# Loading `a` in pairs of chunks for chunks 4 to 11, a third PSUM bank for `b`, and new instruction orders in a scan-plus-adapters kernel

## The chip, the core and the metric

The kernel runs on one core of one Trainium2 chip. A core has a matrix engine (TensorE, PE), a vector engine (VectorE, DVE), a scalar engine (ScalarE, ACT), a general engine (GpSimd, POOL) and a queue engine that here only issues transfers (SyncE, SP); sixteen DMA engines move data between HBM and the on-chip memory. The metric is the device time of one execution in microseconds (us), lower is better. A difference under 0.2%, about 0.4 us here, is hardly to be told from no change.

## The reference

Two inputs `a` and `b`, each 8 sequences of 6,400 rows of 128 numbers, go through a linear recurrence along the sequence. Its output, taken as 51,200 rows `x`, goes through a mixture of eight adapters of rank 16, of which each row uses the two with the largest gate logits:

```python
for t in range(S):
    h = a[:, t] * h + b[:, t]
    out[:, t] = h
...
logits = x @ w_gate                       # 8 logits per row
topk = the two largest per row            # K = 2
w = softmax over those two
delta = sum over the two of w * (x @ A[e]) @ B[e]
return x + delta
```

The two inputs are 26.2 MB each and the output is 26.2 MB, so at least 78.6 MB pass between HBM and the core.

## The kernel before, in words

The 51,200 rows are cut into 100 chunks of 512. A chunk goes through these steps; the letter is the kind of operation as the written orders name it, and the line is that of the profile.

- Load `a` (`x`) and load `b` (`y`), L291, issued by SP (the first `b` by ACT). `LOADS_A` says how many chunks one load of `a` covers: 1 for the first and the last four chunks, 4 for the 92 chunks between. `SEGMENTS` says it for `b`: 1 at both ends, 2 between. A chunk in a load of m is read in rows of 2 KB times m per partition. A tile has four slots of four chunks (`NL`), so loads can be 16 chunks ahead of use; a load waits until its slot's old contents have been transposed.
- Front: PE transposes the chunk so that time lies along the free dimension, L306. A chunk of `a` alone is `a`, a chunk of `b` alone is `b`; between the ends one chunk of `b` and one of `a` that lies ahead are transposed as one group, `f`. With 4-chunk loads, a group for `a` takes one half of the rows of two chunks. ACT copies the transposed `a` out of PSUM (`a`, L342).
- Scan: DVE runs the recurrence of a chunk, reading `a` from SBUF and `b` from PSUM (`s`, L358). Each scan starts from the last column of the one before, so scans are a chain.
- Logits and low-rank products: PE multiplies blocks of 128 rows, up to three at a time, by the 136 columns of A and the gate (`z`, L455) and ACT copies them out (`z`, L462).
- Gating, once for each group in `GROUPS` (1, 1, 2, 2, then 6 chunks, then 4, 2, 2, 1, 1): DVE operations `1`, `2`, `3`, `4`, `6` find the two largest logits (L487 to L503), POOL subtracts (`5`, `8`, L498 and L501), ACT takes one sigmoid (`u`, L507), POOL builds the gates (`p`, `q`, `r`, L516 to L520).
- Back: the products are multiplied by the gates (`m`, L544) on POOL or DVE, as `MU` says for each chunk (82 on POOL, 18 on DVE, these nearly all late); PE transposes two chunks of them (`t`, L552); ACT or DVE copies that out, as `TE` says for each pair (21 on ACT, 31 on DVE, L561); PE adds x and the second product (`d`, L579 and L580); ACT copies the sum out (`o`, L587).
- Store: SP issues the store of one or two chunks (`o` in its own order, L616).

Each engine runs a fixed order, written out in `ORDER` as one letter per operation. An engine takes its operations strictly in that order and waits where an operand is not ready, so a load behind a store in SP's string is issued only once that store's chunk is done. The transfers that SP issues are worked through in the order of issue.

PSUM has eight banks. Two are for transposed `b` (`BANK_B`, banks 1 and 2; a bank is free once its chunk is scanned). Six form a ring (`RING`) that `a`, `f`, `z`, `t` and `d` take in turn; an operation that takes a bank waits for the copy that empties the one six turns back.

The lines that decide which part of `a` goes with which chunk of `b`, before:

```python
if place[0][c][2] == 4 and place[0][c][3] == 0:
    for i in range(4):
        ahead[c + i] = (c + 4 + 2 * (1 - i % 2), i // 2)
```

So `f` of chunk c takes a half of two chunks of `a` from the next 4-chunk load, and a front cannot start before both its `b` and that next load of `a` have landed. The numbers `COLD`, `SOLO`, `FUSED`, `AE` and the `dur` arguments feed the search for the orders; the instructions do not depend on them.

Of the kernel before, what the change touches and what calls it, by code (L numbers as in the profile page):

```python
# [20 lines left out]
ONE_SIGMOID, T_UNIT = True, 2  # L21
RING = [0, 3, 4, 5, 6, 7]
SPLIT = {}
ORDER = {
    "pe": (
        "wwwwwbawwabwzzwwwwbwwazzbaaaazzaztffffzztzfdzzffzzfdfzfzzzffzzftzzffdzfdzzftzfzfzdfdzfzzzfzzfttzzffd"
        "dtddzzfzfdzzfztdffzzdtdffzztdzfdzzfdtzffzztddffzddtdffddzztzffzztzdffzdzztffzzzzdddtdtffzddztffzdzdf"
        "ddfztzzffzdzdtffzzzddftzzzffdztzdftfddzftddffzzzdzfzdftzzffzztzddffdztzdtffzztddffddzzzfdzztzzfzdftz"
        "zfdtdffzzzdddffdtztzffzzzddfdfttzdffazzdztdfddtzzzdzzddtafazdzzbtdzbzztddztdbzzadbdtddzdzdzttddtzddt"
        "dddtdtddddttdd"  # L30
    ),
    "act": (
        "ycciacazzazzuaaaazzuzaataaazztzzauaozzaazozaazzzzaazuatazzaoauzzoztzaazzaoazoazzzzzaauztzaaoooozzaza"
        "ozzazoaazzuootaazozzazoazozaazzutoaoazoouoaaoozzzaazztzoaazzozaazzzzooouoaazooztaazzoooaoazzzuaazzoo"
        "aazzzooazzzaaozztoautaoozaooaazzzoazzouazzaazzzooaaozztoaazzouoaaoozzzaozzzzzaoatzzauooaazzzoooaaozt"
        "zaauzzzaoooatzoaaazzuozooozzzoozzotaauzzzotozzzzoootzzauoouoozzotoztuoooztooooouuoooooo"
    ),
    "dve": (
        "ss12346ss123m4i61ss2s3s4s1s6s2s3s4s6s1s2s3s4s6sss1ss2s3s4sts16s2t3ss4sts1s62s3sts4sts1s263s4stssts6s"
        "ssts1s234tts1s263ss4ssts6sts1s2sts3s41s26s3sts4ss6sts1sts23sts4s6t1s2ssts13s4s2t6s3s4s6stss1s23sts4s"  # L40
        "m6tsts1m2m34s6ss1st12m3m4263s4ts1mm2m63m4mm6t1m21m32m34m4t66tmmtt"
    ),
    "pool": (
        "ccc85qpr85pqrmc855pqrmm8pqrmm85qprmmmm58mmqprmmmmm85mpqrmmmm85mmpqr58mmmmpmqmrmmmm85mmpqrmmm8m5mpqmr"
        "mmmmmm58qprmmm85mmmqprmmmmm58pmqrmmmmmm58pqrmm58mmmmqprmmmm58pqrmmm58qpmrmm58mq85prpq85pqrr8585ppqqr"
        "r"
    ),
    "sp": (
        "xxyxyxyxyxyxyyyxyyxyyxooyxyyoxyyyyyoxxoooyyxoyyyxoyxyooyyxoxoyoyyxoyyxyoooxyoyxyooyxyooyyxooyyxoyyxo"
        "oyxyoooyxoxxyyyoooyooooooooooooooooooo"  # L50
    ),
}
# [105 lines left out]
def bass_associative_scan_2x2__then__mixture_of_adapters_kernel(  # L158
# [21 lines left out]
    span = {}  # L180
    for m in BACKS:
        c0 = len(span)
# [5 lines left out]
    with ExitStack() as stack:  # L188
# [34 lines left out]
        g = sbuf("g", [128, GB, E], F32, NG)  # L223
# [6 lines left out]
        P = Program()  # L230
# [98 lines left out]
        def emptied(c, g, o, ba):  # L329

            ab = c % NA
            m = place[0][c][2]
            if m == 1:
                dst, src = a_st[:, ab, :], lambda: ps[:, ba.n, :]
                chunks = [c]
            else:
                assert ab + 2 <= NA
                dst = a_st[:, ab : ab + 2, :].rearrange("d m t -> d (m t)").rearrange("d (p g j) -> d g p j", g=2, j=8)[:, g, :, :]
                src = lambda: ps[:, ba.n, :].rearrange("d (p j) -> d p j", j=8)
                chunks = [c, c + 1]  # L340
            e = P.add("act", "a", [o] + [ast_user[k % NA] for k in chunks] + [o_sg if c == 0 else None],
                      lambda: eng["act"].copy(dst, src()), dur=AE[0 if m == 1 else 1])  # L342
            ba.evac = e
            for k in chunks:
                o_ae.setdefault(k, []).append(e)
# [26 lines left out]
        for c in range(NCH):  # L372
            if place[0][c][2] == 4 and place[0][c][3] == 0:
                for i in range(4):
                    ahead[c + i] = (c + 4 + 2 * (1 - i % 2), i // 2)

        def solo_a(c, g):
            ba = Bank()
            m = place[0][c][2]
            deps, ts = turned(0, c, ba, g)  # L380
            deps += [w] if c == 2 else []
            o_A[c, g] = P.add("pe", "a", deps, each(ts), dur=SOLO[min(m, 2)] * COLD.get(c, 1), lock=m > 1, ring=ba)
            used(0, c, o_A[c, g])
            emptied(c, g, o_A[c, g], ba)

        def front(c):
            P.at = c
            bb = Bank()
            bb.n = bank_b(c)
            sl, q, m, h = place[0][c]  # L390
            if m == 1:
                solo_a(c, 0)
            elif (c - h, 0) not in o_A:
                for p in (0, 2):
                    for g in (0, 1):
                        solo_a(c - h + p, g)
            deps, ts = turned(1, c, bb)
            deps += user[bb.n]
            if c in ahead and place[0][c + 4][2] == 4:
                c1, g = ahead[c]  # L400
                ba = Bank()
                deps2, ts2 = turned(0, c1, ba, g)
                o = P.add("pe", "f", deps + deps2, each(ts2, ts), dur=FUSED[2], lock=True, ring=ba)
                o_A[c1, g] = o
                used(0, c1, o)
                used(1, c, o)
                o_B[c] = o
                scanned_at(c)
                emptied(c1, g, o, ba)
            elif c in ahead:  # L410
                if h % 2:
                    return
                b2 = Bank()
                b2.n = bank_b(c + 1)
                deps2, ts2 = turned(1, c + 1, b2)
                o = P.add("pe", "f", deps + deps2 + user[b2.n], each(ts, ts2), dur=FUSED[2], lock=True)
                for k in (c, c + 1):
                    used(1, k, o)
                    o_B[k] = o
                    scanned_at(k)  # L420
            else:
                o = P.add("pe", "b", deps, each(ts), dur=SOLO[m] * COLD.get(c, 1))
                used(1, c, o)
                o_B[c] = o
                scanned_at(c)
# [11 lines left out]
        def scanned(b):  # L437
            c0, m = span[b // 4]
            return o_sc[c0 + m - 1]
# [7 lines left out]
        def zlogits(b0, n):  # L447
            P.at = (b0 + n - 1) / 4
            bk = Bank()
            z0 = zpos[b0]  # L450
            assert n <= 3

            def zmm():
                for k in range(n):
                    last = eng["pe"].matmul(ps[:, bk.n, k * W : k * W + W], xblock(b0 + k), Awg_h)  # L455
                return last

            o = P.add("pe", "z", [scanned(b0 + n - 1), o_ch], zmm, dur=(0.059 if span[b0 // 4][1] == 1 else 0.062) * n, ring=bk)
# [111 lines left out]
        def out_chunk(c, e_t):  # L570
# [12 lines left out]
            o_D[c] = P.add("pe", "d", [e_t, o_cB], delta, dur=0.448 if span[c][1] == 1 else 0.48, ring=bo)  # L583
# [39 lines left out]
            o_st.extend(parts)  # L623


        c0 = 0
        behind, due = [], []
        for gi, n in enumerate(GROUPS):
            nb = 4 * n
# [7 lines left out]
            cuts = list(zip(cut, cut[1:]))  # L637
            step = 2 if n % 2 == 0 else 1
            for c in range(c0, c0 + n, step):
                for k in range(c, c + step):  # L640
                    for i, near in ((0, 7), (1, 1)):
                        while loads[i] and loads[i][0][0] <= k + near:
                            load(i, *loads[i].pop(0))
                    front(k)
                while cuts and cuts[0][1] <= 4 * (c + step - c0):
                    k0, k1_ = cuts.pop(0)
                    zlogits(4 * c0 + k0, k1_ - k0)
                for k in range(-(-len(due) * step // (c0 + n - c))):
                    back(*due.pop(0))
# [80 lines left out]
```

## Time and profile before

| | |
|---|---|
| median of 3 runs | 203.28 us (203.04 to 203.30) |
| profiled execution | 203.03 us, of which its span is 201.2 us |
| PE / DVE / ACT / POOL busy | 179.9 / 177.1 / 178.2 / 127.4 us |
| moved by DMA | 79.28 MB, mean 394 GB/s over the span |
| mean granted PE clock | 0.987 |

The profile is of one execution, the one of 203.03 us. Its span runs from the first to the last instruction or transfer; 1.8 us of the execution's time lie outside it. Times in the rows below are us from the start of the span. A row of a group gives busy time, the mean of one instruction in ns, and the idle time of the engine just before. A row of the stretches view gives, for each engine, busy us and in brackets the number of instructions, then the granted PE clock, the share of the sixteen DMA engines that was busy, and GB/s. A row of the issues view gives the size of one transfer and the median time from its issue to its landing, that is until the last of the sixteen engines has delivered its part.

### The profile page before, as it was taken

The numbers are of one execution on the slowest core, as the hardware profiler recorded it, in microseconds if no ns is written. First come the engines' busy times: TensorE is split into PE (matmuls) and PEld (weight loads), VectorE is DVE, ScalarE is ACT, GpSimd is POOL, SyncE is SP. The second block draws the span as 40 slices with busy tenths as digits, with TensorE's granted clock in tenths as the row PEclk, the third lists the DMA queues.
The fourth block names the chain that finished last, engine by engine and source line by source line (L and its number), as shares of the span: only waits on it lengthen the run. The fifth ranks groups of instructions, "written<-read, shape, count | busy, mean of one in ns | idle before, by whom it ended". The sixth has DMA issues, their size and how long they took to land.

```text
span 201.2 us, 7662 instructions
## 1 busy us (share of the span) xinstructions
PE 179.9 (89%) x3150; PEld 164.3 (82%) x3150; DVE 177.1 (88%) x269; ACT 178.2 (89%) x384; POOL 127.4 (63%) x205
## 2 busy tenths in 40 slices
PE   4986788899989998999999999899999999898880
PEld 3975676788989998899999998789989898897760
DVE  0587689999989998999999999898999999999860
ACT  2376597999999999999999999899999999999970
POOL 1024006692797979785998697678788885865420
PEclk9999699999999999999999999999999999999998
DMA  6999999999999999999999999999999999998596
GB/s 189 396 410 414 414 410 412 416 421 396 419 415 419 409 411 423 410 423 406 419 418 405 418 415 415 416 415 414 422 410 411 415 407 404 418 360 346 234 357 226
DMA packets 21379, 79.28 MB, mean 394 GB/s; under 512 B 3424, under 2 KB 3552, under 8 KB 18400
## 3 DMA queue, kind: packets, MB, share of 16 engines
q1 hardware_dynamic: 19872, 78.39, 96.5%
q10 hardware_dynamic: 1472, 0.40, 0.9%
q8 instruction: 25, 0.41, 0.9%
q14 instruction: 10, 0.08, 0.1%
HBM read 52.56 MB, written 26.21 MB: 391 GB/s over the span
## 4 chain that ended last, share of the span: by engine, by line
PE 51%; DVE 17%; DMA 16%; ACT 5%; issue 4%; SPq 3%; POOL 2%; ACTq 0%
PE ps L306 20%; DMA b_tm<-in_b_dram 16%; DVE xT L358 10%; PE ps L455 10%; PE ps L579 8%; PE ps L552 7%; PE ps L580 6%; DVE zw L544 3%; ACT outt L587 3%; SPq L291 3%; ACT zl L462 1%; DVE zwT L561 1%; POOL g L518 1%; DVE L L492 1%; DVE k L490 0%
## 5 line engine op out<-in xcount | busy, mean ns | idle before, releaser
L358 DVE TENSOR_TENSOR_SCAN xT<-a_st,xT,ps 128x512 f16<-128x512 f32 x96 | 120.2, 1253 | 7.4 <-PE ps L306 5.3
L544 POOL TENSOR_TENSOR zw<-zl,g 128x512 f16<-128x512 f32 x82 | 85.9, 1069 | 9.9 <-PE ps L552 8.6
L306 PE MATMUL ps<-ident_f,a_tm 64*128 64x64 f32 (+1 forms) x768 | 66.3, 232 | 6.6 <-DVE xT L358 2.4
L462 ACT COPY zl<-ps 128x408 f32<-128x408 f32 (+1 forms) x138 | 67.9, 596 | 4.7 <-PE ps L455 4.5
L342 ACT COPY a_st<-ps 128x512 f32<-128x512 f32 x100 | 62.9, 691 | 7.3 <-PE ps L306 6.9
L306 PE MATMUL ps<-ident_f,b_tm 64*128 64x64 f32 (+1 forms) x768 | 66.0, 233 | 2.8 <-DMA b_tm<-in_b_dram 1.5
L306 PEld LDWEIGHTS ps<-ident_f,a_tm 64*128 64x128 f32 (+1 forms) x768 | 55.9, 141 | 13.0 <-issue 3.0
L587 ACT COPY outt<-ps 128x512 f32<-128x512 f32 x100 | 61.5, 691 | 2.9 <-PE ps L580 2.3
L306 PEld LDWEIGHTS ps<-ident_f,b_tm 64*128 64x128 f32 (+1 forms) x768 | 54.9, 141 | 4.4 <-issue 2.4
L579 PE MATMUL ps<-ident_h,xT 128*128 128x128 f16 x400 | 57.3, 231 | 0.6 <-ACT zwT L561 0.4
L580 PE MATMUL ps<-cst_h,zwT 128*128 128x128 f16 x400 | 55.7, 220 | 1.7 <-issue 1.7
L579 PEld LDWEIGHTS ps<-ident_h,xT 128*128 128x128 f16 x400 | 49.5, 142 | 3.9 <-ACT zwT L561 0.9
L580 PEld LDWEIGHTS ps<-cst_h,zwT 128*128 128x128 f16 x400 | 42.7, 107 | 1.1 <-issue 1.1
L455 PE MATMUL ps<-cst_h,xT 128*128 128x136 f16 x400 | 41.7, 232 | 1.3 <-DVE xT L358 0.9
L455 PEld LDWEIGHTS ps<-cst_h,xT 128*128 128x128 f16 x400 | 32.2, 145 | 4.2 <-DVE xT L358 1.4
L552 PE MATMUL ps<-ident_h,zw 128*128 128x128 f16 x400 | 30.8, 219 | 1.4 <-DVE k L490 0.6
L552 PEld LDWEIGHTS ps<-ident_h,zw 128*128 128x128 f16 x400 | 23.9, 98 | 3.3 <-ACT outt L587 0.8
L561 ACT COPY zwT<-ps 128x1024 f16<-128x1024 f16 (+1 forms) x21 | 21.7, 1033 | 0.0
L561 DVE COPY zwT<-ps 128x1024 f16<-128x1024 f16 (+1 forms) x31 | 20.3, 658 | 1.2 <-PE ps L552 1.2
L518 POOL TENSOR_TENSOR g<-k,w 128x192 f32<-128x192 f32 (+3 forms) x23 | 10.7, 467 | 11.4 <-DVE k L503 9.5
L498 POOL TENSOR_TENSOR dd<-m 128x24 f32<-128x24 f32 (+3 forms) x23 | 5.8, 251 | 16.5 <-DVE m L496 16.5
L501 POOL TENSOR_TENSOR dd<-m 128x24 f32<-128x24 f32 (+3 forms) x23 | 6.0, 259 | 15.1 <-DVE m L496 15.0
(23 smaller groups left out, 90.2 us busy)
## 6 DMA issues: line engine op xcount, KB each, us to landing
a_tm<-in_a_dram SPq DMA_DIRECT2D x23, 1024.0 KB, 16.4
b_tm<-in_b_dram SPq DMA_DIRECT2D x46, 512.0 KB, 16.8
out_dram<-outt SPq DMA_DIRECT2D x46, 512.0 KB, 14.4
a_tm<-in_a_dram SPq DMA_DIRECT2D x8, 256.0 KB, 9.7
out_dram<-outt SPq DMA_DIRECT2D x8, 256.0 KB, 5.2
b_tm<-in_b_dram SPq DMA_DIRECT2D x7, 256.0 KB, 11.8
b_tm<-in_b_dram ACTq DMA_DIRECT2D x1, 256.0 KB, 3.6
cst_f<-in_moe_A_dram ACTq DMA_DIRECT2D x1, 64.0 KB, 4.3
```

What stands on the lines that cost most here:

```text
L306: return [lambda k=k: eng["pe"].transpose(dv(k), src[r, 8 * g + k, :], ident_f[r, r]) for k in range(n)]
L342: lambda: eng["act"].copy(dst, src()), dur=AE[0 if m == 1 else 1])
L358: last = eng["dve"].tensor_tensor_scan(out=xT[:, xb, s0:s1], data0=a_st[:, c % NA, s0:s1], data1=ps[:, bk, s0:s1], initial=init, op0=ALU.m ...
L455: last = eng["pe"].matmul(ps[:, bk.n, k * W : k * W + W], xblock(b0 + k), Awg_h)
L462: lambda: eng["act"].copy(zl[:, z0 : z0 + n, :].rearrange("p k w -> p (k w)"), ps[:, bk.n, 0 : n * W]),
L518: lambda: eng["pool"].tensor_tensor(out=gg, in0=kk2, in1=bc(u2), op=ALU.mult), dur=pd)
L544: lambda me=me, wv=wv, zv=zv, gv=gv: eng[me].tensor_tensor(out=wv, in0=zv, in1=gv, op=ALU.mult),
L552: last = eng["pe"].transpose(ps[:, bt.n, :].bitcast(F16)[:, k * 128 : k * 128 + 128], zw[:, w + k // 4, k % 4, :], ident_h[:, :])
L561: f = (lambda: eng["act"].copy(dst, src())) if te == "act" else (lambda: eng["dve"].tensor_copy(dst, src()))
L579: eng["pe"].matmul(dst, xblock(b0 + k), ident_h[:, :], start=True, stop=False)
L580: last = eng["pe"].matmul(dst, zwT[:, w, k * 128 : k * 128 + 128], B_h, start=False, stop=True)
L587: lambda: eng["act"].copy(outt[:, p0 : p0 + 4, :].rearrange("p k d -> p (k d)"), ps[:, bo.n, :]), dur=0.6)
```

## The change

The loads of `a` for chunks 4 to 11 cover two chunks each (four loads of 512 KB in place of two of 1 MB). For these chunks, `f` of chunk c takes the whole chunk c+1 of `a`; from chunk 8 on, `f` takes its half of the next 4-chunk load as before, and chunks 4, 9, 10 and 11 of `a` are transposed alone. `b` has three PSUM banks, 0, 1 and 2, and the ring has five, 3 to 7. The fronts of two chunks that share a load are recorded together. All five orders, and the lists `TE` and `MU`, are new: `t` is copied 19 times by ACT and 33 times by DVE, `m` runs 85 times on POOL and 15 times on DVE. PE's counts of each kind stay as they were (12 `a`, 90 `f`, 8 `b`, 138 `z`, 52 `t`, 100 `d`); SP has two more loads of `a`.

```diff
-LOADS_A = [1] * 4 + [4] * 23 + [1] * 4
+LOADS_A = [1] * 4 + [2] * 4 + [4] * 21 + [1] * 4
...
-BANK_B = [1, 2]
+BANK_B = [0, 1, 2]
...
-COLD, SOLO, FUSED, AE = {0: 1.95, 1: 1.3}, {1: 0.436, 2: 0.48}, {2: 0.59}, [0.592, 0.592]
+COLD, SOLO, FUSED, AE = {0: 1.95, 1: 1.3}, {1: 0.436, 2: 0.48}, {2: 0.50}, [0.592, 0.61]
...
-RING = [0, 3, 4, 5, 6, 7]
+RING = [3, 4, 5, 6, 7]
...
     "dve": (
...
-        "m6tsts1m2m34s6ss1st12m3m4263s4ts1mm2m63m4mm6t1m21m32m34m4t66tmmtt"
...
+        "sstsssts1s2m3t41263t4ss12mmm36s4s162mmm3m4t1m2m634t12m3m466tmmtt"
     ),
...
     "sp": (
-        "xxyxyxyxyxyxyyyxyyxyyxooyxyyoxyyyyyoxxoooyyxoyyyxoyxyooyyxoxoyoyyxoyyxyoooxyoyxyooyxyooyyxooyyxoyyxo"
-        "oyxyoooyxoxxyyyoooyooooooooooooooooooo"
+        "xxyyxyxyxxyxxxyyxyyxyyyxyxoyoyyxoyyxoxyoyyoyxyooxyyoxoyyyooxyyxooyyxyyxooooyyxyyooxoyyxoyoyxoyyoxooy"
+        "oxoyoyxxxyoyyooooxoyoyooyooooooooooooooo"
     ),
...
 TE = (
-    "aaaadaddaddaddadddadddaadddadddaddaadddaadadaadadddd"
+    "aaaaaaddaddddaddddaaddddddddaadddddadddaddaaaaddaddd"
 )
 MU = (
-    "dpppppppppppppppppppppppppppppppppppppppppppppppppppppppppppppppppppppppppppdpdpdppppddpdddddddddddd"
+    "pdppppppppppppppppppppppppppppppppppppppppppppppppppppppppppppppppppppppppppppppppdpppddpddddddddddd"
 )
...
             m = place[0][c][2]
-            if m == 1:
+            if m < 4:
                 dst, src = a_st[:, ab, :], lambda: ps[:, ba.n, :]
                 chunks = [c]
...
-                    ahead[c + i] = (c + 4 + 2 * (1 - i % 2), i // 2)
+                    ahead[c + i - 4] = (c + 2 * (1 - i % 2), i // 2)
...
-            sl, q, m, h = place[0][c]
-            if m == 1:
+            if c not in o_ae:
                 solo_a(c, 0)
-            elif (c - h, 0) not in o_A:
-                for p in (0, 2):
-                    for g in (0, 1):
-                        solo_a(c - h + p, g)
             deps, ts = turned(1, c, bb)
             deps += user[bb.n]
-            if c in ahead and place[0][c + 4][2] == 4:
-                c1, g = ahead[c]
+            m = place[1][c][2]
+            if m > 1 and (c in ahead or place[0][c + 1][2] == 2):
+                c1, g = ahead.get(c, (c + 1, 0))
                 ba = Bank()
                 deps2, ts2 = turned(0, c1, ba, g)
                 o = P.add("pe", "f", deps + deps2, each(ts2, ts), dur=FUSED[2], lock=True, ring=ba)
...
-                for k in range(c, c + step):
+                for k in range(nf, span[c + step - 1][0] + span[c + step - 1][1]):
+                    nf = k + 1
```

More of the change, by code (lines that the diff above doesn't have):

```diff
@@ L24 @@
 ORDER = {
     "pe": (
[L26 to L30, printed above, removed]
+        "wwwwwwwwbawwwawbwwzabzzzbazaffzztfzzfzaafffafzzzdzftzzzfztfzzfffdzdzfzftzzzfdfffzzdzzfzfzzztffzdztff"
@@ L341, in emptied @@
             e = P.add("act", "a", [o] + [ast_user[k % NA] for k in chunks] + [o_sg if c == 0 else None],
-                      lambda: eng["act"].copy(dst, src()), dur=AE[0 if m == 1 else 1])
+                      lambda: eng["act"].copy(dst, src()), dur=AE[m // 4])
             ba.evac = e
@@ L409, in front @@
                 emptied(c1, g, o, ba)
-            elif c in ahead:
-                if h % 2:
+            elif m > 1:
+                if c in o_B:
                     return
@@ L456, in zmm @@
                 return last
-            o = P.add("pe", "z", [scanned(b0 + n - 1), o_ch], zmm, dur=(0.059 if span[b0 // 4][1] == 1 else 0.062) * n, ring=bk)
+            o = P.add("pe", "z", [scanned(b0 + n - 1), o_ch], zmm, dur=ZD[span[b0 // 4][1]] * n, ring=bk)
             for k in range(n):
@@ L581, in delta @@
                 return last
-            o_D[c] = P.add("pe", "d", [e_t, o_cB], delta, dur=0.448 if span[c][1] == 1 else 0.48, ring=bo)
+            o_D[c] = P.add("pe", "d", [e_t, o_cB], delta, dur=DD[span[c][1]], ring=bo)
             reads(b0, o_D[c])
@@ L623, in store @@
             o_st.extend(parts)
-        c0 = 0
+        nf, c0 = 0, 0
         behind, due = [], []
```

23 lines of the change are left out of this document (14 added, 9 removed).

## The prediction

> **What bounds the kernel now.** I read the page of the profile first, then the stretches of the span, then the chain of work that ended last, then single issues of SP with their time to landing.
>
> ```profile
> span 201.2 us, 7662 instructions
> PE 179.9 (89%) x3150; PEld 164.3 (82%) x3150; DVE 177.1 (88%) x269; ACT 178.2 (89%) x384; POOL 127.4 (63%) x205
> DMA  6999999999999999999999999999999999998596
> GB/s 189 396 410 414 414 410 412 416 421 396 419 415 419 409 411 423 410 423 406 419 418 405 418 415 415 416 415 414 422 410 411 415 407 404 418 360 346 234 357 226
> q1 hardware_dynamic: 19872, 78.39, 96.5%
> PE 51%; DVE 17%; DMA 16%; ACT 5%; issue 4%; SPq 3%; POOL 2%; ACTq 0%
> a_tm<-in_a_dram SPq DMA_DIRECT2D x23, 1024.0 KB, 16.4
> b_tm<-in_b_dram SPq DMA_DIRECT2D x46, 512.0 KB, 16.8
> out_dram<-outt SPq DMA_DIRECT2D x46, 512.0 KB, 14.4
> ```
>
> No engine of the core is above 89%, while the queue of loads and stores is at 96.5% of what the sixteen DMA engines have, and the row of DMA tenths is 9 from the second slice to the 36th. The table of stretches says it by stage:
>
> ```profile
> 15.00:20.00 5.00, 3.05 (x71) 2.55 (x69) 3.67 (x7) 3.23 (x7) 2.35 (x7) 1.00 1.03 416
> 20.00:25.00 5.00, 3.90 (x48) 3.44 (x48) 3.53 (x6) 2.67 (x7) 0.37 (x2) 0.69 1.02 411
> 60.00:125.00 65.00, 64.15 (x1243) 59.53 (x1241) 63.56 (x86) 64.66 (x142) 52.56 (x72) 1.00 1.02 415
> 160.00:175.00 15.00, 13.98 (x224) 13.30 (x221) 14.86 (x21) 14.86 (x34) 10.79 (x18) 1.00 1.03 409
> 175.00:185.00 10.00, 9.28 (x140) 8.79 (x139) 10.00 (x25) 9.63 (x23) 5.78 (x12) 1.00 0.91 361
> 185.00:200.00 15.00, 9.80 (x144) 8.38 (x142) 8.79 (x25) 9.52 (x20) 4.71 (x17) 0.98 0.77 300
> 200.00:200.50 0.50, 0.00 (x0) 0.00 (x0) 0.00 (x0) 0.00 (x0) 0.00 (x0) 0.50 0.04 16
> ```
>
> The DMA share is 1.02 or 1.03 up to 175 us, at 409 to 416 GB/s, in the early stretches too where DVE and ACT stand idle for a third of the time. Only after 175 us does the mean share fall. Half a microsecond before the end it is 0.04 of sixteen engines, 0.6 of one: a single DMA engine, behind the others, ends the kernel.
>
> ```profile
> 4.10 0.44 SPq L291
> 6.83 15.16 DMA b_tm<-in_b_dram
> 22.03 1.12 PE ps L306 x15
> ...
> 141.31 17.86 DMA b_tm<-in_b_dram
> 159.22 1.80 PE ps L306 x36
> ...
> 180.74 1.26 DVE xT L358
> 182.11 1.20 DVE zw L544 x2
> 195.33 1.17 ACT outt L587 x2
> ```
>
> In this chain, two loads of `b` take 15.2 and 17.9 us from issue to landing; most of it is waiting behind other transfers, since the least that any store needs here is 3.4 us (row below). PE starts the front of chunk 8 at 22.03, 0.04 us after that chunk's `b` landed. The last scan starts at 180.74, and the last copies into `outt` end at 196.50.
>
> ```profile
> 164.29 1.06 SPq L291 DMA_DIRECT2D b_tm<-in_b_dram  x1
> b_tm<-in_b_dram SPq DMA_DIRECT2D x1, 256.0 KB, 12.5
> 178.44 0.61 PE L306 MATMUL ps<-ident_f,b_tm 128*128 128x128 f32 x4
> 195.94 1.26 SPq L616 DMA_DIRECT2D out_dram<-outt  x2
> out_dram<-outt SPq DMA_DIRECT2D x2, 256.0 KB, 4.1
> DMA to landing us min/median/max: 3.4/12.8/19.2
> ```
>
> The load of the last chunk of `b` is issued at 164.29 and lands 12.5 us later, at 176.8; PE transposes it at 178.44. The last store is issued at 196.6 and lands 4.1 us later, at 200.7, 0.7 us more than the least (3.4, for a store twice as large). So the end still has a little queue ahead of it: the DMA stream and the last copies of the core end nearly together, with about 0.7 us of room on the core's side.
>
> **The change, part by part.**
>
> *Smaller early loads.* In SP's string, the loads that stand ahead of `b` of chunk 8 are `a` 0 to 15 and `b` up to 7, before and after: the same bytes. Chunks 4 to 7 can start earlier (`f` of chunk 4 no longer needs `a` 8 to 11), but chunk 8 cannot: its `b` lands at about 22.0 in both. From there on a front needs the same loads as before, and a stream that is never empty delivers them at the same pace. So what the head wins (up to the 1.3 us that DVE and 1.8 us that ACT stand idle in 15 to 20 us) is waited away at 22 us. I take 0. The two more issues on SP cost 0.44 us each and stand in front of a load that waits 15 us anyway: 0. If the queue ran dry behind them they would cost 0.9 us. PE's clock of 0.69 in 20 to 25 us follows the stretch in which PE works 3.05 of 5 us; the wait for chunk 8 stays, so I expect the dip to stay, off the path.
>
> *Rows of 4 KB in place of 8 KB.* 2.1 MB are read in shorter rows. The stretches run at 409 to 416 GB/s whatever the mix of sizes; 2.1 MB at the one instead of the other is 5.13 against 5.04 us. Between -0.1 and +0.1; I take +0.1, as shorter rows will hardly be faster. In the Trainium skill, "DMA: Bandwidth & Descriptors", section "Rules for kernel authors", the row on maximum bandwidth asks for at least 1 MiB per DMA, and this change halves two such loads. By the fixed cost of about 2.0 us per DMA that the skill fits (section "Anatomy of one DMA", measured for DMAs that GpSimd issues), two more would be an estimated 4.0 us if nothing hid it, and the sum would be 207.7 instead of 203.7. The trace speaks against it: two thirds of its bytes (92 transfers of 512 KB against 23 of 1 MB) move in halves of that size, and the stream holds 415 GB/s.
>
> *Banks.*
>
> ```profile
> PE ps L306 <- DVE xT L358: 3.1, 5, 1.0
> PE ps L306 <- ACT outt L587: 0.3, 1, 0.3
> L544 DVE TENSOR_TENSOR zw<-zl,g 128x512 f16<-128x512 f32 x18 | 12.9, 730 | 0.7 <-POOL g L520 0.7
> L561 DVE COPY zwT<-ps 128x1024 f16<-128x1024 f16 x29 | 19.5, 674 | 1.0 <-PE ps L552 1.0
> L561 ACT COPY zwT<-ps 128x1024 f16<-128x1024 f16 x19 | 20.5, 1078 | 0.0
> L544 POOL TENSOR_TENSOR zw<-zl,g 128x512 f16<-128x512 f32 x82 | 85.9, 1069 | 9.9 <-PE ps L552 8.6
> ```
>
> A third bank for `b` can take away at most the 3.1 us that PE waits for scans. The ring with one bank less adds waits for the copies that empty it; the trace has few (0.3 us for `o`), and a new wait would hold PE's queue: the next `z`, `t` and `d`, and ACT and DVE behind them. Bounds -3.1 and +3.1 us, on PE. I take 0 on the path: before 175 us the loads set the pace, and a front that is late by less than the loads' waiting (15 to 18 us) frees its slot in time. Without that cover it would be the whole amount.
>
> *Moved copies.* ACT loses two `t` (2 x 1.08 = 2.2 us); DVE gains two (2 x 0.67) and loses three `m` (3 x 0.73), so -0.8 us; POOL gains 3 x 1.07 = 3.2 us, with 127 us busy of 201. Before 175 us this is beside the stream: 0. What of it stands at the end is counted next.
>
> *The tail.* Here SP's order moves something. Behind the last load of `b` (the last `y`) stood 15 double and 4 single stores, 34 chunks; now 11 and 4, 26 chunks. So eight more chunks, 8 x 0.262 = 2.1 MB, go ahead of that load: at 361 to 409 GB/s 5.1 to 5.8 us, I take 5.4. It lands at 182.2 rather than 176.8, and PE cannot transpose it at 178.44 any more; the operations behind it in PE's string (`d` of chunk 84 first) wait with it, and ACT's copies for them. The total of the stream does not change by this, since as much less is left behind the load.
>
> The last scan then starts a front later, 182.2 + 0.6 = 182.8, against 180.74: +2.1. Behind the last scan DVE had 12 `m`, 5 `t` and 16 gating operations; now 10, 5 and 16. Two `m` less are 1.2 us (the row of the chain: two in 1.20). So DVE, and with it the last copies, end 2.1 - 1.2 = 0.9 us later, at 197.4. Of this 0.7 us fall into the room that the last store had (4.1 against 3.4). What is left is +0.2 us. The bounds: 0 if the room is a little larger, and +3.1 if the work behind the last load is as long as before (182.2 - 178.44 = 3.8, less 0.7).
>
> Sum against the profiled execution: 203.03 + 0.1 + 0.2 = 203.3. Its time is 0.25 us under the median of the runs shown, so against the median the same sum is 203.28 + 0.3 = 203.6. As the tail's unknowns lie nearly all on the late side (the next stores, of chunks 84 to 91, have ACT's copies behind later `d` too), I set 203.7.
>
> **The rivals.**
>
> *Slower: the tail's work does not shrink with the time left for it.* Place: PE, ACT and DVE after the last load has landed. It decides once the last copy into `outt` ends later than 196.5 + 0.7 = 197.2. Price: from +0.8 us to the bound of 3.1; 204.1 to 206.4. For it: in 175 to 185 us DVE works 10.00 of 10 us and ACT 9.63, so a late start is not easily made good. Against it: in 185 to 200 DVE works only 8.79 of 15 and ACT 9.52, so the last stretch is latency and order more than work, and new orders may pack it better.
>
> *Faster: the engines are the bound, not the stream.* Then the lighter ACT and DVE decide, at -2.2 and -0.8 us, and the earlier start of chunks 4 to 7 carries through: 201.1 to 202.5, say 202.1. For it: PE, DVE and ACT work 64.15, 63.56 and 64.66 of 65 us in 60 to 125, and PE has 51% of the chain. Against it: the DMA share is 1.02 in the same stretch, and the chain enters PE from loads at 22 and at 159 us. It also has little to win at the end: at 200.0 only one DMA engine is still at work, and earlier copies do not make that engine faster.
>
> *The fixed cost of more, smaller loads shows.* Two more loads of a queue that ran in series: 2 x 3.4 us (the least time of a transfer here) is +6.8 at most. The rate of 415 GB/s with 15 us of queue excludes nearly all of it. With one or both in full it would be 207.0 to 210.4, with little chance.
>
> **How the numbers follow.** A difference under 0.2%, 0.4 us, can hardly be told from none. The forecast, the stream as it was with a tail up to 0.8 us later, 203.0 to 204.1: 0.50, of which 0.28 within 0.2% and 0.22 slower. The slower tail: 0.25. The engines as the bound: 0.22, faster. The fixed cost: 0.03. So faster 0.22, same 0.28, slower 0.50. The likeliest case's own range is 203.0 to 204.1; for 8 in 10 it has to reach into both rivals: 202.1 to 205.6.
>
> **What the profile of the changed kernel would show.** The front of chunk 8 at 22.0 within 0.5 us, with the chain coming from the load of `b`; DMA share at or above 1.0 in every stretch of 5 us from 10 to 175; the last load of `b` landing at 181.5 to 183, with PE's last front of `b` right behind; last copies into `outt` ending at 197 to 198; the last store landing 3.4 to 4.1 us after its issue. A DMA share clearly under 1 before 175 us, or a last load that lands by 178, would make the argument wrong; last copies before 196.5 together with an earlier end would speak for the engines as the bound.

## The result and the profile after

The changed kernel takes 204.04 us (median of 7 runs, 203.74 to 204.08). The kernel before took 203.28 us beside it. The ratio is 1.0033, with a 95% interval of 1.0021 to 1.0045: 0.76 us slower by the medians. The profiled execution of after took 204.04 us with a span of 202.2 us, against 203.03 and 201.2. Of the runs below, three of the twelve executions of experiment 6 took 204.3 to 204.4 us in a second, slower state and are left out of its ratio. Behind the head of the program, the line numbers of after are one higher up to the scans (L307 front, L343 copy of `a`, L359 scan) and three lower after them (L541 `m`, L558 `t`, L584 `o`, L613 stores).

The stretches of after, to be held against those of before:

```profile
15.00:20.00 5.00, 3.70 (x63) 3.00 (x62) 4.74 (x13) 3.69 (x9) 1.42 (x6) 1.00 1.03 411
20.00:25.00 5.00, 3.12 (x55) 3.07 (x55) 3.13 (x5) 2.41 (x7) 4.19 (x12) 0.71 1.01 411
...
60.00:125.00 65.00, 61.68 (x1175) 56.75 (x1174) 61.22 (x83) 61.38 (x133) 49.96 (x68) 1.00 1.02 415
...
160.00:175.00 15.00, 13.93 (x236) 13.02 (x233) 14.35 (x17) 13.79 (x31) 13.47 (x15) 1.00 1.03 410
175.00:185.00 10.00, 8.98 (x127) 8.26 (x127) 9.69 (x19) 8.47 (x18) 7.18 (x15) 1.00 0.87 347
185.00:200.00 15.00, 11.61 (x171) 9.96 (x168) 11.94 (x32) 12.21 (x26) 5.68 (x19) 1.00 0.74 289
```

The stream of transfers is as full as before up to 175 us (share 1.01 to 1.03). DVE does more by 20 us (4.74 of 5 us in 15 to 20), and less in the middle (61.22 of 65, before 63.56). By the starts of the fronts, after is 3.2 us ahead at chunk 34 (60.51 against 63.69) and 2.4 us behind at chunk 64 (115.56 against 113.12): the head was won, and the lead was gone by the middle. In 185 to 200 PE, DVE and ACT have more left to do than before (DVE 11.94, before 8.79).

The chain of waits of after, the pieces that enter an engine from a load, and three of the tail:

```profile
7.38 14.51 DMA b_tm<-in_b_dram
21.93 4.13 PE ps L307 x62
...
140.85 18.42 DMA b_tm<-in_b_dram
159.31 0.73 PE ps L307 x12
...
183.23 1.19 DVE xT L359
...
197.85 1.14 ACT outt L584 x2
```

The first load is that of `b` 8, as before: the head still ends there, at 21.93. The second is that of `b` 88. In before the second entry of the chain was `b` 90, at the same time (159.22). So at 159.3 us after is one pair of chunks behind. The front of `b` 90 follows at 162.08, 2.86 us later than in before.

The timeline of after: SP's issues of the loads of `b` 88 and of the last `b`, PE's front of that last `b`, DVE's last two scans, SP's issue of the last store; and below it the issues view of the same three transfers:

```profile
140.85 1.59 SPq L292 DMA_DIRECT2D b_tm<-in_b_dram  x1
168.56 1.28 SPq L292 DMA_DIRECT2D b_tm<-in_b_dram  x1
182.09 0.66 PE L307 MATMUL ps<-ident_f,b_tm 128*128 128x128 f32 x4 [0.17 <-DMA b_tm<-in_b_dram]
183.15 1.27 DVE L359 TENSOR_TENSOR_SCAN xT<-a_st,xT,ps 128x512 f16<-128x512 f32 x1
184.52 1.28 DVE L359 TENSOR_TENSOR_SCAN xT<-a_st,xT,ps 128x512 f16<-128x512 f32 x1
199.01 0.33 SPq L613 DMA_DIRECT2D out_dram<-outt  x1
```

```profile
b_tm<-in_b_dram SPq DMA_DIRECT2D x1, 512.0 KB, 18.4
b_tm<-in_b_dram SPq DMA_DIRECT2D x1, 256.0 KB, 13.5
out_dram<-outt SPq DMA_DIRECT2D x1, 256.0 KB, 2.6
```

The last load lands at 182.1 (168.56 + 13.5) and PE transposes it at once, after waiting only 0.17 us for it. The last scan starts at 184.52 (before 180.74), the last copies into `outt` end at 198.99 (before 196.50). The last store lands 2.6 us after its issue instead of 4.1. So the core is 2.5 us later, the end of the queue 1.5 us shorter, and about 1.0 us is left in the span.

### The profile page after: what moved, and what is told of

It is laid out like the page before. It is cut to its first block, busy times and chain, and to the rows that moved or that the text cites. A ratio compares the mean times of both kernels' runs of the same rounds, so it can differ in the third digit from the quotient of the medians.

```text
span 202.2 us, 7644 instructions
## 1 busy us (share of the span) xinstructions
PE 180.9 (89%) x3150; PEld 164.7 (81%) x3150; DVE 179.8 (89%) x268; ACT 177.9 (88%) x382; POOL 130.4 (64%) x208
## 4 chain that ended last, share of the span: by engine, by line
PE 42%; DVE 17%; DMA 16%; ACT 15%; issue 3%; SPq 3%; POOL 2%; DVEq 0%
PE ps L307 18%; DMA b_tm<-in_b_dram 16%; DVE xT L359 8%; PE ps L576 7%; PE ps L452 6%; PE ps L549 6%; PE ps L577 5%; DVE zw L541 4%; ACT a_st L343 4%; ACT outt L584 4%; ACT zl L459 4%; SPq L292 3%; ACT zwT L558 3%; DVE zwT L558 2%; DVE L L489 1%
## 5 line engine op out<-in xcount | busy, mean ns | idle before, releaser
L359 DVE TENSOR_TENSOR_SCAN xT<-a_st,xT,ps 128x512 f16<-128x512 f32 x96 | 120.3, 1253 | 6.5 <-PE ps L307 3.5
L541 POOL TENSOR_TENSOR zw<-zl,g 128x512 f16<-128x512 f32 x85 | 89.6, 1079 | 11.8 <-PE ps L549 10.7
L307 PE MATMUL ps<-ident_f,a_tm 64*128 64x64 f32 (+1 forms) x768 | 65.3, 234 | 5.3 <-DMA b_tm<-in_b_dram 2.4
L459 ACT COPY zl<-ps 128x408 f32<-128x408 f32 (+1 forms) x138 | 64.9, 558 | 2.1 <-PE ps L452 2.0
L307 PE MATMUL ps<-ident_f,b_tm 64*128 64x64 f32 (+1 forms) x768 | 64.8, 233 | 1.3 <-DMA b_tm<-in_b_dram 1.0
L343 ACT COPY a_st<-ps 128x512 f32<-128x512 f32 x100 | 58.7, 648 | 8.1 <-PE ps L307 7.2
L307 PEld LDWEIGHTS ps<-ident_f,a_tm 64*128 64x128 f32 (+1 forms) x768 | 55.9, 143 | 11.4 <-DMA b_tm<-in_b_dram 2.7
L584 ACT COPY outt<-ps 128x512 f32<-128x512 f32 x100 | 58.2, 646 | 3.8 <-PE ps L577 3.6
L307 PEld LDWEIGHTS ps<-ident_f,b_tm 64*128 64x128 f32 (+1 forms) x768 | 54.6, 142 | 2.1 <-DMA b_tm<-in_b_dram 1.6
L558 DVE COPY zwT<-ps 128x1024 f16<-128x1024 f16 (+1 forms) x33 | 21.7, 659 | 3.6 <-PE ps L549 3.4
L515 POOL TENSOR_TENSOR g<-k,w 128x192 f32<-128x192 f32 (+3 forms) x23 | 10.6, 459 | 13.9 <-DVE k L500 10.1
L558 ACT COPY zwT<-ps 128x1024 f16<-128x1024 f16 (+1 forms) x19 | 19.3, 1024 | 0.1
L495 POOL TENSOR_TENSOR dd<-m 128x24 f32<-128x24 f32 (+3 forms) x23 | 5.4, 241 | 17.1 <-DVE m L493 17.1
L498 POOL TENSOR_TENSOR dd<-m 128x24 f32<-128x24 f32 (+3 forms) x23 | 5.2, 230 | 12.9 <-DVE m L493 12.6
## 6 DMA issues: line engine op xcount, KB each, us to landing
b_tm<-in_b_dram SPq DMA_DIRECT2D x46, 512.0 KB, 15.8
b_tm<-in_b_dram SPq DMA_DIRECT2D x7, 256.0 KB, 13.5
```

The source lines that it names most:

```text
L307: return [lambda k=k: eng["pe"].transpose(dv(k), src[r, 8 * g + k, :], ident_f[r, r]) for k in range(n)]
L343: lambda: eng["act"].copy(dst, src()), dur=AE[m // 4])
L359: last = eng["dve"].tensor_tensor_scan(out=xT[:, xb, s0:s1], data0=a_st[:, c % NA, s0:s1], data1=ps[:, bk, s0:s1], initial=init, op0=ALU.m ...
L459: lambda: eng["act"].copy(zl[:, z0 : z0 + n, :].rearrange("p k w -> p (k w)"), ps[:, bk.n, 0 : n * W]),
L515: lambda: eng["pool"].tensor_tensor(out=gg, in0=kk2, in1=bc(u2), op=ALU.mult), dur=pd)
L541: lambda me=me, wv=wv, zv=zv, gv=gv: eng[me].tensor_tensor(out=wv, in0=zv, in1=gv, op=ALU.mult),
```

## The experiments

Two theories ran through them. The *stream theory*, that of the prediction: the stream sets the pace up to 175 us, then the last load of `b` and what is behind it. The *engine theory*: DVE, and with it PE and ACT, have no room, so the time is their work. From experiment 9 on a third one stood beside them: the stream holds PE back at one place only, the fronts of chunks 88 and 90, and what follows is a fixed length of work. In the expectations the engine theory is called that of DVE.

All runs in one table. "Front" is the start of the front of chunk 88 (of 90 for before and its variants), "copies" the end of the last copies into `outt`, both from the profiled execution.

| kernel | ratio to before, 95% | span | front | copies | copies - front |
|---|---|---|---|---|---|
| before | | 201.2 | 159.22 | 196.50 | 37.28 |
| after | 1.0033 (1.0021 to 1.0045) | 202.2 | 159.31 | 198.99 | 39.68 |
| after, tail of before's SP order | 1.0263 (1.0248 to 1.0278) | 206.4 | | 203.26 | |
| before, tail of after's SP order | 1.0270 (1.0244 to 1.0295) | 207.2 | | | |
| before, banks of after | 1.0100 (1.0080 to 1.0120) | 203.1 | 159.50 | 198.83 | 39.33 |
| before, loads of after | 1.0438 (1.0414 to 1.0463) | 210.5 | | | |
| after, DVE work added | 1.0100 (1.0073 to 1.0128) | 202.9 | 160.03 | 199.77 | 39.74 |
| after, two stores less | 0.9942 (0.9921 to 0.9963) | 199.8 | 156.79 | 196.72 | 39.93 |
| after, last loads first | 1.0046 (1.0031 to 1.0061) | 202.0 | 159.25 | 198.91 | 39.66 |
| after, scans before copies | 1.0055 (1.0041 to 1.0069) | 202.1 | 159.31 | 198.97 | 39.66 |
| before, `b` 90 late | 1.0174 (1.0150 to 1.0199) | 205.0 | 161.67 | 200.36 | 38.69 |
| after, DVE's tail | 1.0037 (1.0021 to 1.0053) | 201.9 | 159.37 | 198.69 | 39.32 |
| after, banks undone | 1.0541 (1.0508 to 1.0575) | 211.7 | | 208.50 | |
| after, tail retimed | 1.0027 (1.0013 to 1.0042) | 201.7 | 159.29 | 198.53 | 39.24 |

**1 and 2: the tail of SP's order swapped.** After with the 27 entries of before between two points at which both orders have issued the same transfers; and before with those of after.

```diff
 "sp" of after, entries 99 to 125
-oyoxoyoyxxxyoyyooooxoyoyooy
+yyxooyxyoooyxoxxyyyoooyoooo
```

> The changed kernel with one thing undone: SP's order of the last 27 entries before the final stores, in which the kernel before has eight more chunks of stores behind the last load of b. Theory 1, the late last loads make the tail late: the last b lands at about 177 instead of 182.0, the last copies into outt end at 197.0 to 197.5 instead of 199.0, the DMA share in 185 to 190 us rises from 0.42 to 0.6 or more, and the time falls from 204.0 to 203.0 to 203.5. Theory 2, the new orders of DVE, ACT and POOL at the end (with collisions of DVE and POOL) make it late: the loads land earlier but the last copies still end at 198.5 to 199.2, time 203.8 to 204.2. Theory 3, the smaller loads or the banks cost it: 203.8 to 204.2 too.

> The kernel before with the same 27 entries of SP's order taken from the changed kernel, all else as it was. Theory 1: the last b lands at about 182, the last copies end at 197.5 to 199, time 203.8 to 204.6. Theories 2 and 3: the time stays at 203.1 to 203.5.

Both were far slower, which no theory expected. In the first the last load of `b` landed at 176.3, 5.7 us sooner than in after, and the kernel still took 4.2 us more. Its waits between 145 and 165 us, and its stretch from 155 to 160:

```profile
ACT outt L584 <- DMA out_dram<-outt: 3.6, 2, 3.4
```

```profile
155.00:160.00 5.00, 2.68 (x25) 2.30 (x27) 1.06 (x5) 2.95 (x7) 0.00 (x0) 0.73 1.03 419
```

`outt` holds 16 chunks. A copy `o` waits until the store from 16 chunks ago has landed; with loads put ahead of stores ACT waits 3.4 us for one, and behind it, in order, everything stops while the DMA share stays at 1.03. In the second kernel the load of `b` 88 lands at 158.9, much as in after (159.3), where before had its front at 155.4; PE waits 3.3 us for it. So loads can't be drawn ahead freely: the stores of chunk c have to land before the copies of c+16. And a stop of 3.4 us at 156 came out as 4.2 us at the end. The engines did not make it up. Because of these stops the two runs do not answer what they were made for.

**3: the banks alone, in before.**

```diff
-BANK_B = [1, 2]
+BANK_B = [0, 1, 2]
-RING = [0, 3, 4, 5, 6, 7]
+RING = [3, 4, 5, 6, 7]
```

> The kernel before with three PSUM banks for b and five in the ring, all orders as they were. Theories 1 and 2: 203.1 to 203.5, PE's waits for scans fall from 3.1 us to under 1.5, the waits for banks of the ring rise by about as much, all beside the stream. Theory 3 (banks): 203.7 to 204.2, with PE waiting for copies of ACT near the end.

1.0% slower, 204.89 us, which is more than any of the theories expected. The fronts reach chunk 90 as before (159.50 against 159.22). The loss comes behind: the scan of chunk 92 starts at 167.41 instead of 165.95, that of 94 at 173.27 instead of 171.81. The wait of PE's fronts for scans, 3.1 us in before, is gone, and others stand in its place (fronts for ACT's copies of `a` 0.9 us, PE's `d` for `o` 0.8 us, DVE for `t` 0.5 and 0.7 us at 166 and 182 us). With before's orders a ring of five costs more than the third bank brings.

**4: the loads alone, in before.** The loads in pairs for chunks 4 to 11 and the program of after, with two banks for `b`, six in the ring and before's orders; what must differ was placed by hand.

```diff
 "sp"
-xxyxyxyxyxyxyyyxyy...
+xxyxyxyxxyxxyxyyyxyy...
 "pe"
-bwwazzbaaaazzaztffffzztzfdzzffzzfdf
+bwwazzbaazzztffffzztzfdzzafafzzafdf
 "act"
-uaaaazzuzaataaazztzzauaozzaa
+uaaaazzuzaatzzatzzaaauoazzaa
```

> The kernel before with only the loads of a for chunks 4 to 11 in pairs: SP issues two loads in each place where it issued one of 1 MB, the three solo fronts of a (chunks 9 to 11) move behind the fronts that need them first, with the first copies of ACT moved to match, all else as before. Theories 1 and 2: front of chunk 8 still at 22.0, time 203.1 to 203.6. Theory 3 (fixed cost of a load): two more loads in series cost 2 to 6 us, 205 or more.

4.4% slower, and no test of the loads: its stretches show that the hand-placed order stalls the head.

```profile
15.00:20.00 5.00, 2.51 (x36) 2.13 (x36) 0.69 (x5) 2.35 (x6) 1.06 (x5) 0.50 1.02 415
...
30.00:35.00 5.00, 2.88 (x36) 2.27 (x35) 2.76 (x4) 2.85 (x7) 0.00 (x0) 0.69 0.55 218
```

DVE works 0.69 of 5 us, and at 30 us the stream itself runs dry (0.55) because no slot comes free: between 15 and 45 us two loads wait on SP for PE's transposes, 21.2 us together. What the shorter rows cost by themselves is read from the traces instead (below).

**5: more work on DVE in the middle of after.**

```diff
+burn = sbuf("burn", [128, 1], F32)
+last = o_id
+for k in range(8):
+    last = P.add("dve", "D", [o_id, last], lambda: eng["dve"].tensor_reduce(burn[:, 0:1], ident_f[:, :], ...))
 "dve": DDDDDDDD behind the scan of chunk 50
```

> After, with eight reductions of 128x128 added on DVE behind the scan of chunk 50 (0.28 us each by the row of L493, 128x16<-128x128, so 2.2 us; nothing reads them). Stream theory (the forecast's: the DMA stream sets the pace up to 175 us, then the last load of b): the scans of chunks 51 and later are late by 2.2 us at first, but the loads have 4.6 us of lead at chunk 50 and 0.0 at chunk 88, so the lateness is gone by 160 us; 204.0 to 204.4. DVE theory (DVE has no room from 25 us to its last copy: idle 5.1 us of 172 in after): the whole of it arrives at the end, 205.8 to 206.6.

Between the two. The timeline has the addition:

```profile
92.28 2.51 DVE L271 TENSOR_REDUCE burn<-ident_f 128x1 f32<-128x128 f32 x8
```

The front of chunk 60 is 2.3 us late against after (107.87 and 105.56), that of chunk 64 1.0 us (a pause of DVE at 110 us in after is used up), that of 88 0.72 us, and the last copies 0.78 us. So two thirds of the addition vanish before 160 us, and nothing of the rest vanishes after it. By the ratios it cost 0.67% (1.0100 against 1.0033), 1.4 us, twice as much. Its six executions spread from 203.86 to 206.13, and the profiled one is not undisturbed either: PE's clock in 10 to 25 us was 0.73 against 0.90 in after, ahead of the addition. So the size of what is left is uncertain, between 0.7 and 1.4 us of 2.5.

**6: two stores less in the middle of after.**

```diff
 def store(c, n):
+    if 30 <= c < 34:
+        return
```

> After, without the two stores of chunks 30 to 33 (those rows of the output are not written; 1 MB, 2.5 us of the stream at 415 GB/s, in the middle of the run). Stream theory: everything behind them comes 2.5 us earlier, the last load of b at 179.5 instead of 182.0; 201.3 to 202.0. DVE theory: the loads come earlier but DVE cannot use it, except for the 0.5 us for which it waits at 159.9 and 165.9; 203.4 to 204.1.

The stream theory's time: 2.4 us less by the span, 0.9% (1.8 us) by the ratios. The front of chunk 88 comes 2.5 us sooner and the last copies 2.3 us sooner. At that place the stream sets the pace. It does so by little: behind the head the trace shows no wait of PE for a load any more, `b` 88 lands at 156.6 and its front starts at 156.79, so the engines are next in line.

**7: the last loads of after sooner.**

```diff
 "sp" of after, from the load of b 94
-yyooooxoyoyooyo
+yyooxyyyooooooo
```

> After, with the loads of a 99 and b 97, 98, 99 moved in SP's string ahead of the stores of chunks 62 to 73 (loads up to b 96 stay where they are). The last load of b then lands at about 176 instead of 182.0. Stream theory with the late load as the cause of the loss: the tail is as long as before, 202.4 to 203.3. DVE theory: DVE works without a pause from 166 to 194 in after and its order is unchanged, so the last scan starts at the same 184.5 and the time stays, 203.8 to 204.3.

The time of after. Timeline: the issues of `b` 98 and 99, the last front, the last scans, the last copies:

```profile
160.18 1.86 SPq L292 DMA_DIRECT2D b_tm<-in_b_dram  x2
181.69 0.61 PE L307 MATMUL ps<-ident_f,b_tm 128*128 128x128 f32 x4
183.09 1.27 DVE L359 TENSOR_TENSOR_SCAN xT<-a_st,xT,ps 128x512 f16<-128x512 f32 x1
184.47 1.28 DVE L359 TENSOR_TENSOR_SCAN xT<-a_st,xT,ps 128x512 f16<-128x512 f32 x1
197.78 1.13 ACT L584 COPY outt<-ps 128x512 f32<-128x512 f32 x2 [0.76 <-PE ps L577]
```

The last load lands at 173.9, 8.1 us sooner, and the last scan starts 0.05 us sooner. The late last load of `b`, on which the prediction's sum rests, cost nothing: DVE comes to the last scan at the same time, whether its load has landed 10.6 us before or 2.5.

**8: DVE's idle places of the middle removed.**

```diff
 "dve" of after
-... s48 t31 s49 ...  3 t41 t43 4 s62 ...
+... s48 s49 t31 ...  3 s62 t41 t43 4 ...
```

> After, with DVE's order changed at two places of the middle: the scan of chunk 49 ahead of the copy of zwT of chunk 31, and the scan of chunk 62 ahead of the copies of chunks 41 and 43. These are where DVE stands idle for 0.79 us (88.7) and 1.13 us (110.2) waiting for PE's transposes. Stream theory: 0, since the loads decide again at 160 us; 203.8 to 204.2. DVE theory: up to 1.9 us less, 202.2 to 203.2.

No gain: by the medians the time of after (204.08 and 204.04), by the ratios, each against before measured beside it, 0.2% above it (1.0055 and 1.0033). Two pauses of 1.9 us are gone, others come in their place (0.79 us at 91.9, 0.67 at 115.0), and the front of 88 starts at 159.31, to the hundredth as in after. What is won before that front is lost at it. Experiments 7, 10 and 12, whose engines have the orders of after up to 155 us, say the same: their profiled executions start the front of 64 at 113.2 to 113.9, that of after at 115.56, and the front of 88 comes at 159.25 to 159.37 in all four.

**9: before with `b` 90 late.** The reverse test: two stores are put ahead of that load, as in after.

```diff
 "sp" of before, from the load of a 92
-xooyxyoooy
+xooooyxyoy
```

> Before, with one edit in SP's string: the stores of chunks 52 to 55 are issued ahead of the load of b 90 instead of behind that of b 92, as in after. The load of b 90 then lands 2.5 us later (161.7 instead of 159.2), that of b 92 too; the last load of b stays at 176.8. Theory of the front at 159 us (the stream holds PE back at that place only, and from there to the last copy PE, ACT and DVE have a fixed amount of work): all of it arrives at the end, 205.0 to 205.7. The forecast's theory (the last load of b and what is behind it): nothing changes, 202.8 to 203.5.

1.7% slower (206.57 us), above both ranges, and more than the 2.5 us by which the load was delayed. The chain of waits, and DVE's timeline behind it:

```profile
143.63 17.99 DMA b_tm<-in_b_dram
161.67 2.33 PE ps L306 x36
```

```profile
162.42 1.28 DVE L358 TENSOR_TENSOR_SCAN xT<-a_st,xT,ps 128x512 f16<-128x512 f32 x1 [2.71 <-PE ps L306]
166.51 0.69 DVE L544 TENSOR_TENSOR zw<-zl,g 128x512 f16<-128x512 f32 x1 [1.38 <-PE ps L552]
```

The front starts 2.45 us later, and DVE, whose order was made for the earlier front, stands idle once more for 1.38 us. Together 3.8 us, which is what the last copies are late (200.36 against 196.50).

**10: DVE's tail in after.**

```diff
 "dve" of after, near the end
-s2m3t41263t4ss12mmm36s4s162
+s2mt341263t4ss12mmsm36s4162
```

> After, with DVE's order changed at two places behind 165 us: the copy of zwT of chunk 79 ahead of the gating operation that took 1.22 us instead of 0.35 beside POOL's multiplication, and the scan of chunk 98 ahead of the multiplication that took 1.54 us instead of 0.68, with the scan of 99 ahead of one gating operation. If DVE sets the pace behind 166 us: up to 0.9 + 0.9 us less, 202.2 to 203.3. If the other engines' orders hold the tail: 203.7 to 204.2.

No gain beyond the interval. The two operations are shorter and the last scan starts 1.5 us sooner, but then DVE waits:

```profile
173.58 0.62 DVE L489 SCALAR_TENSOR_TENSOR L<-k,zl 128x192 f32<-128x192 f32 x1
...
182.99 1.27 DVE L359 TENSOR_TENSOR_SCAN xT<-a_st,xT,ps 128x512 f16<-128x512 f32 x1
...
185.33 0.22 DVE L484 TENSOR_REDUCE m<-zl 128x8 f32<-128x64 f32 x1 [0.96 <-POOL g L517]
```

It waits for gates that POOL builds, in its order, only behind a subtraction that needs DVE's operation `4`, and I had put that behind the scan. DVE's work was not what held the tail alone.

**11: the banks undone in after.** The lists of experiment 3, reversed.

> After, with the PSUM banks as before (two for b, six in the ring), all orders as in after. If the banks are worth nothing, as the forecast has it, and waits ahead of 159 us are absorbed there: 203.8 to 204.3. If the third bank of b is what lets the fronts of after run ahead of the scans: fronts behind 159 us wait for scans, up to the 3.1 us that PE waited for scans in before: 204.5 to 207.

5.4% slower than before, 9.5 us longer than after by the spans, and more than the worst I expected. PE's waits, first in after, then here:

```profile
PE ps L307 <- DVE xT L359: 0.3, 1, 0.3
```

```profile
PE ps L307 <- DVE xT L359: 8.1, 13, 1.6
```

With two banks the front of chunk c waits for the scan of c-2. After's orders let the fronts run three ahead; take the bank away and 13 fronts stop PE, and everything queued behind them.

**12: a retimed tail.** SP's edit of experiment 7 with `b` 92 ahead of `a` 96 to 98, and:

```diff
 "pe" of after
-taazazfzdd
+tfaazazzdd
 "dve" of after
-s2m3t41263t4ss12mmm36s4s162
+s2mt341263t4ss12mms364ms162
```

> After, with its orders behind 155 us changed: the load of b 92 ahead of those of a 96 to 98 and PE's front of 92 ahead of those of a 96 to 98 (takes away DVE's 0.33 us at 165.9); the last four loads ahead of the stores of chunks 62 to 73; the copy of chunk 79 and the scan of 98 ahead of the two operations that were held up beside POOL (0.9 us each); and three gating operations ahead of the scan of 99, so that POOL, and ACT which waits for it at 185.0, go on about 1.2 us sooner. The front of 88 stays at 159.3, as the stream sets it. If the time is the work of the engines from that front on: 0.8 to 1.8 us less than after, a ratio to before of 0.995 to 1.000. If the front of 88 alone decided it, whatever the order behind it: as after, a ratio of 1.002 to 1.005.

The ratio is 1.0027, inside after's interval; the last copies are 0.46 us sooner. That is the second theory's range and short of the 0.8 us of the first: shortening waits behind the front of 88 hardly paid. It beats neither kernel.

## Why the prediction was right, and where it was not

The forecast was 203.7 us, with 203.0 to 204.1 for its likeliest case; measured were 204.04. The number holds, at the upper end. The path to it holds in the first half and fails in the second. That the number came so near is in part luck: two errors of the tail, of 1.6 and 0.8 us, have opposite signs.

*The head is neutral: right.* The front of chunk 8 starts at 21.93 (forecast 22.0), out of the load of `b`, PE's clock dips there as before (0.71, before 0.69), and what DVE gained in 15 to 20 us did not reach the end. Experiment 8 shows why such a gain is lost, at a place I had not named: it is waited away at chunk 88.

*Shorter rows cost at most 0.1 us: right.* `b` 8 has the same bytes ahead of it in both kernels, in after with two more loads and half the row length for 2.1 MB. It landed at 21.89 (7.38 + 14.51) against 21.99 (6.83 + 15.16). The estimate of 4.0 us for two more loads, worked out from the fixed cost in the Trainium skill's "DMA: Bandwidth & Descriptors", section "Anatomy of one DMA", is not borne out in this queue, which is never empty (share 1.03 in 15 to 20 us). Experiment 4, meant for this, told nothing.

*Banks cost nothing: wrong as a price of that part.* The lists of banks alone cost 1.0% with before's orders (experiment 3), and undoing them costs 9.5 us with after's (experiment 11), beyond my bound of 3.1 us. Banks and orders have no prices of their own; only the pair has one.

*Moved copies cost nothing before 175 us: in line with the runs, not tested alone.* What DVE won before the front of 88 in experiment 8 was taken back there.

*The tail: the step that failed.* I let the last load of `b` decide: its landing at 182.2 (measured 182.1), a front and a scan behind it, two `m` less, last copies at 197.4. Landing and front came as forecast, and so did what lies behind the last scan: from its start to the last copies 14.5 us in after against 15.8 in before, 1.3 us less (forecast 1.2). But the last scan started 3.8 us later than in before, not 2.1, the last copies ended at 198.99, and experiment 7 shows that the landing has no part in it. The runs put another mechanism in its place. The front at which the stream last sets the pace is that of chunk 90 in before, at 159.22; in after it is that of 88 at 159.31, with 90 at 162.08. From the front of 90 to the last copies the core needs 37.3 us in before and 36.9 in after. In the seven kernels with after's PE and bank structure whose front of 88 starts anywhere from 156.8 to 160.0, the rest from the front of 88 on is 39.2 to 39.9 us. So after's last copies are late by 2.86 - 0.37 = 2.5 us, with the front of 90.

That front is late because the front of 88 is. PE's fronts of 88 and 90 in after, then in experiment 6, where no load holds PE:

```profile
159.31 0.27 PE L307 MATMUL ps<-ident_f,a_tm 64*128 64x64 f32 x1 [0.48 <-DMA b_tm<-in_b_dram]
162.08 0.24 PE L307 MATMUL ps<-ident_f,a_tm 64*128 64x64 f32 x1
```

```profile
156.79 0.27 PE L307 MATMUL ps<-ident_f,a_tm 64*128 64x64 f32 x1
159.43 0.27 PE L307 MATMUL ps<-ident_f,a_tm 64*128 64x64 f32 x1
```

With no load in the way the front of 90 follows 2.64 us after that of 88 (2.63 in experiment 5), in after 2.77 us; `b` 90 landed there at 162.0 (issued at 142.99, 19.0 us to landing), so its own landing cost about 0.1 us. The front of 88 starts 3.87 us later than in before (155.44). Its load is issued, in after, behind the stores of chunks 48 to 53 (1.6 MB, 3.8 us of the stream at 415 GB/s), which in before stand behind that load and behind the load of `a` 92 that the same front needs. Experiment 9 shows in before that a delay of the load for which PE waits reaches the end; it moved other stores, those of chunks 52 to 55, ahead of `b` 90. That the place of the stores of 48 to 53 accounts for all of after's 2.5 us is argued from the traces and not shown: no run moves them alone, and the outright reverse in after runs into the ring of `outt` (experiment 1).

I saw that eight more chunks of stores stood ahead of the last load of `b`. The question to ask of SP's order was which load a front is waiting for. The time from the landing of `b` to its front answered that for before: 0.05 us at chunk 90, 1.7 us at the last. It is not enough by itself: in after `b` 86 to 94 all land 0.05 to 0.4 us ahead of their fronts, and the last `b` 0.04 us, which cost nothing.

*The room at the end: too small.* I gave the last store at least 3.4 us, the least seen in before, so 0.7 us of room. It took 2.6 us, so the room was 1.5. The two errors have opposite signs: copies 1.6 us later than forecast, landing 0.8 us quicker.

*The rivals.* The slower one came about as a mechanism: its condition (last copies later than 197.2) is met by 1.8 us, and its reason, that the tail's work does not shrink, is what the table shows. Its price of at least 0.8 us was just missed (0.76 measured, 204.04 against its 204.1), since the landing gave 0.8 us more back. The faster one, engines as the bound, is half true. From about 156 us on hardly anything is made good (experiments 1, 5 and 9), but before that the stream takes back what the engines win (8) and sets when the front of 88 can start (6). That more and smaller loads show a fixed cost is not borne out by `b` 8.

## What to carry to other kernels

Where a full stream and full engines run side by side, look for the last place at which the stream sets an engine's pace: what the engines gain before it is lost, and from it on nearly every delay reaches the end. To find it, take for each load the time from landing to first use; where that is near zero the load may be what counts. Then ask whether what follows waits for that load too: the last `b` of after was used 0.04 us after it landed, and bringing it 8.1 us sooner gained 0.05 us, as DVE came to its scan 2.4 us after the front had started in any case. Orders, banks and buffer rings that were searched together have no separate prices: five swaps of one part alone (experiments 1, 2, 3, 4 and 11) all came out 1.0 to 5.4% above before, more than the whole change, though experiment 4 had operations placed by hand.

## What was not expected of the hardware

Some elementwise operations of DVE with two operands in SBUF stand still while POOL multiplies. POOL's timeline of after, then DVE's:

```profile
172.37 1.57 POOL L541 TENSOR_TENSOR zw<-zl,g 128x512 f16<-128x512 f32 x1 [0.23 <-PE ps L549]
```

```profile
172.32 0.69 DVE L541 TENSOR_TENSOR zw<-zl,g 128x512 f16<-128x512 f32 x1
172.93 1.22 DVE L489 SCALAR_TENSOR_TENSOR L<-k,zl 128x192 f32<-128x192 f32 x1
```

POOL's multiplication, 1.06 us when alone, starts 0.05 us after DVE's and takes 1.57; DVE's next operation, 0.35 us by the median, takes 1.22 and ends 0.2 us after POOL's. The times fit that one waits for the other to finish, and not that both slow down. In experiment 10, with the copy of a transposed tile (PSUM to SBUF) between, the copy took its usual 0.68 us beside POOL and the operation 0.62. In experiment 12 the sides change: POOL's operation of 0.41 us takes 0.85, ending behind DVE's multiplication.

```profile
183.17 0.85 POOL L515 TENSOR_TENSOR g<-k,w 128x128 f32<-128x128 f32 x1 [0.86 <-DVE m L493]
```

The Trainium skill, "SBUF — State Buffer", section "SBUF: two separate sides", says this of a DVE operation with two SBUF inputs beside a GpSimd operation that reads SBUF: the pair of ports that they share is held for the whole instruction by whichever starts first, and the other blocks. The trace agrees, with 0.4 to 0.9 us for each meeting; the prediction had no term for it.

A store of 256 KB lands 2.6 us after its issue in after; in before the same store took 4.1. The share of the stretch from 185 to 190 us was 0.42 in after and 0.65 in before, so in after the queue had been emptier shortly before. That this is the reason is not shown; at the very end the DMA engines were busier in after (0.92 from 199 to 200 us) than in before (0.33 from 199.0 to 199.5, 0.09 behind it). In any case the smallest time of one profile is no floor: it was 3.4 us in before, 2.6 in experiments 3 and 9 and 2.5 in after.
